# A hand-ordered mixer kernel on one core: new delays for small transfers in its planner, a new order list, sets numbered through the batches

## The chip, the core and the metric

The kernel runs on one core of a Trainium2 chip. Time is device time in microseconds (us) of that core, from one launch. Engines are named as in the profile: PE is TensorE (PEld its weight loads), DVE is VectorE, ACT is ScalarE, POOL is GpSimd, SP is the engine that here only issues transfers. POOL, too, issues transfers, through the software queue.

## The reference

For each of 4 batches, a gated linear attention of 8 heads (sequence 768, head size 48) is followed by a token mixer and a channel mixer with shared weights:

```python
f = 1 / (1 + exp(-f_logit))                       # (B, H, S, D)
for t in range(S):
    state = f[:, :, t, :, None] * state + k[:, :, t] (outer) v[:, :, t]
    y[:, :, t] = q[:, :, t] @ state
x = y as (B, S, H*D)                              # H*D = 384
xt = x.transpose(0, 2, 1)
u = x + (relu(xt @ w_tok1) @ w_tok2).transpose(0, 2, 1)   # 768 -> 256 -> 768
out = u + relu(u @ w_ch1) @ w_ch2                 # 384 -> 1536 -> 384
```

Inputs and output are float32; the kernel computes its matrix products in bfloat16 with float32 accumulation.

## The kernel before, in words

The sequence is cut into 6 chunks of 128 rows. In the text "b.c" is chunk c of batch b, as in sums3.4. For each chunk the kernel makes these steps, each one an entry of a plan:

- gates (L443): ACT takes exp and ln of the loaded f, and DVE or POOL (L457) the low half "Llo" of the logarithm.
- sums (L516): a matmul with a triangle of ones adds the logarithms along the chunk; ACT makes the factors G and Gi (L541, L543), and for batches 1 to 3 "ends" (L550), whose last row a 2 KB transfer "glast" (L556, issued by SP) spreads over the partitions.
- DVE multiplies q and k by the factors (L562) into one of four sets qk. The set is turned (128x128 transposes) into qkT: for batches 0 to 2 on PE (L579) with a copy by DVE or ACT, for batch 3 (TURNED) by a transfer that transposes (L569, issued by SP).
- scores (L476) are made on PE from qkT, and masked into AmT (L616, DVE); "parts" (L492) multiply k by v; DVE carries the running state (L628 to L633), which is copied into state_bd ("sbd", L639) by ACT or POOL.
- y (L651 and L658) makes the chunk's output from state and AmT; it is copied into x_bf and x_nat (L680).

Then the mixer of the batch follows: tok1 (L693), a relu copy, tok2 (L709), the sum (L725) and u_bf (L737); u_bf is turned into uT in two halves "th", on PE (L750) for batches 0 and 1 and by transposing transfers (L739, SP) for batches 2 and 3 (U_TURNED); ch1 (L768) with relu copies into zT (L439 on ACT, L441 on DVE); ch2 (L787), whose sum with x_nat (L793, DVE) is stored by SP (L797), 192 KB at a time. The last tile of the last batch is split into columns 0 to 288 and 288 to 384. x_nat has three buffers, so batch 3 writes into the buffer of batch 0 once that was stored.

Nothing of this runs in the order in which it is written. Every step is added to a list of 1116 entries. ORDER names each entry once, as 4 times its index plus the number of the engine chosen among those that it allows. Plan.best walks through ORDER with prices and landing times written into the entries, chooses a PSUM bank for each user, puts filler matmuls (L834) on PE where it sees PE idle for over 250 ns before 25.5 us, and emits the steps sorted by planned start. On one engine that is the order of ORDER. The planned times are in no instruction: on the chip each engine takes its own list in order, and waits on semaphores for what an instruction needs. So what the plan decides is the order on each engine, the engine of each step, the banks and the fillers.

Entry kinds: ("mm", ...) is PE work, ("el", ...) an elementwise step, ("load", ...) an input transfer, ("fix", own, till) a step that holds its engine for own ns and is done after till ns. Three kinds of ("fix", ...) entries had a fourth number before, by which they took a share of a modelled wire (L235 to L238): glast, the turning transfers and the stores.

Of the kernel before, what the change touches and what calls it, by code (L numbers as in the profile page):

```python
# [20 lines left out]
TURNED = 3  # L21
ORDER = (
# [60 lines left out]
)  # L83
KEPT = 3
SPLIT = 5
SLOTS = (5110, 5800, 7500, 8450, 9600, 10400, 11400, 13000, 14400, 14800, 16700,
         18000, 19100, 19500, 20000, 20700, 21400, 23400, 24300, 25900)
HELD = (2600, 3600, 4100, 4750, 5500, 6500)


class Op:
# [162 lines left out]
def kernel(  # L254
# [25 lines left out]
    def st(shape, dtype, tag):  # L280
        return sb.tile(shape, dtype, tag=tag, name=tag)
# [586 lines left out]
```

## Time and profile before

| what | value |
|---|---|
| runs | 172.79, 171.46, 176.41 us; median 172.79 |
| span of the profiled execution | 170.2 us (the record has its span; a time of its own is not listed) |
| granted TensorE clock in the profile | 1.00 |
| instructions | 4181 |
| PE, DVE, ACT, POOL busy | 162.9, 128.0, 108.2, 99.3 us |
| filler matmuls (L834) | 30 |

The page gives busy time of each engine, the chain of work that ended last, groups of instructions with what ended the idle time before them, and transfers with their time from issue to landing. A matmul's busy time covers its way through the array, so consecutive matmuls overlap in it: how fast PE works is read from the distance of their starts, which the chain of work shows as pieces with a count ("7.80 PE ps L768 x48").

### The profile page before, as it was taken

The page shows a single profiled execution, that of the slowest core. Times are in us where ns is not written, and L with a number is a line of the kernel's source. Part 1 is how long each engine was busy: PE and PEld are TensorE (multiplying, and loading weights), DVE is VectorE, ACT ScalarE, POOL GpSimd, SP SyncE. Part 2 cuts the span into 40 slices and gives each one's busy share as a digit, 9 for nine tenths or more (in the row PEclk, how much of TensorE's full clock was granted, in tenths as well). Part 3 has the DMA queues.
Part 4 walks back from the last instruction along what each step waited for, and adds up shares of the span by engine and source line. Part 5 has one row for each costly group of instructions (what it writes and reads, how often), then busy time and mean ns, then how long its engine had stood idle before and what let it go on. Part 6 is the DMA issues. An engine that isn't in the chain of part 4 may idle for free.

```text
span 170.2 us, 4181 instructions
## 1 busy us (share of the span) xinstructions
PE 162.9 (96%) x1606; PEld 102.8 (60%) x1606; DVE 128.0 (75%) x287; ACT 108.2 (64%) x256; POOL 99.3 (58%) x134
## 2 busy tenths in 40 slices
PE   6899999999999999999999999999999999999992
PEld 2356565665766576665776756665666666566661
DVE  5679995966898998899999868768884723675431
ACT  4759993598879889999999978385545320510100
POOL 7999569896499969999978869603111200000000
PEclk9999999999999999999999999999999999999999
DMA  6999999999999997999998999996920060220253
GB/s 103 141 174 149 156 192 181 212 149 201 192 167 136 161 165 75 116 155 133 182 157 49 134 251 107 144 165 115 228 100 4 0 139 0 92 96 0 78 202 139
DMA packets 102547, 22.71 MB, mean 133 GB/s; under 512 B 95264, under 2 KB 101664, under 8 KB 102528
## 3 DMA queue, kind: packets, MB, share of 16 engines
q0 software_dynamic: 79440, 13.77, 101.8%
q1 hardware_dynamic: 22560, 8.59, 22.5%
q8 instruction: 12, 0.20, 0.5%
q10 hardware_dynamic: 528, 0.10, 0.3%
q14 instruction: 7, 0.06, 0.1%
HBM read 25.17 MB, written 4.72 MB: 176 GB/s over the span
## 4 chain that ended last, share of the span: by engine, by line
PE 64%; DMA 12%; DVE 7%; ACT 6%; POOL 6%; issue 2%; SPq 1%; DVEq 0%; POOLq 0%
PE ps L768 22%; PE ps L787 22%; DMA v_sb<-in_v_dram 5%; PE ps L709 4%; POOL qk_sb L360 4%; PE ps L693 4%; DMA glast<-ends 4%; DMA out_dram<-x_nat 3%; DVE AmT L616 2%; PE ps L476 2%; PE ps L579 2%; PE ps L658 2%; POOL v_sb L360 1%; PE ps L530 1%; PE ps L651 1%
## 5 line engine op out<-in xcount | busy, mean ns | idle before, releaser
L787 PE MATMUL ps<-w_ch,zT 128*128 128x384 bf16 (+2 forms) x300 | 51.6, 320 | 0.0
L768 PE MATMUL ps<-uT,w_ch 128*128 128x384 bf16 x288 | 50.6, 326 | 0.0
L439 ACT ACTIVATE zT<-ps 128x384 bf16<-128x384 f32 x56 | 25.3, 494 | 25.3 <-PE ps L768 25.2
L768 PEld LDWEIGHTS <-w_ch 128*128 128x128 bf16 x288 | 27.7, 98 | 17.7
L787 PEld LDWEIGHTS <-zT 128*128 128x128 bf16 x300 | 27.9, 98 | 16.9
L616 DVE TENSOR_TENSOR AmT<-ps,tri_bf 128x512 bf16<-128x512 f32 x46 | 30.5, 686 | 2.5 <-PE ps L476 2.3
L441 DVE TENSOR_SCALAR zT<-ps 128x384 bf16<-128x384 f32 x40 | 21.1, 554 | 8.8 <-PE ps L768 8.8
L360 POOL DMA_DIRECT2D v_sb<-in_v_dram x24 | 22.2, 925 | 4.1 <-DMA w_ch<-in_moe_w_ch_dram 4.1
L360 POOL DMA_DIRECT2D qk_sb<-in_k_dram x24 | 22.4, 932 | 0.8 <-POOLq L852 0.8
L360 POOL DMA_DIRECT2D qk_sb<-in_q_dram x24 | 22.3, 930 | 0.0
L793 DVE TENSOR_TENSOR x_nat<-x_nat,ps 128x384 f32<-128x384 f32 (+2 forms) x25 | 13.3, 535 | 10.6 <-PE ps L787 10.2
L360 POOL DMA_DIRECT2D f_sb<-in_f_logit_dram x18 | 16.5, 943 | 0.2
L562 DVE TENSOR_TENSOR qk<-qk_sb,GG 128x768 bf16<-128x768 bf16 (+1 forms) x30 | 14.2, 475 | 2.1 <-ACT GG L543 1.0
L450 ACT ACTIVATE f_sb<-f_sb 128x384 f32<-128x384 f32 x24 | 12.5, 524 | 4.6 <-DMA f_sb<-in_f_logit_dram 4.4
L434 POOL CAST state_bd<-state 48x192 bf16<-48x192 f32 x13 | 4.5, 347 | 16.2 <-DVE state L633 14.6
L725 DVE TENSOR_TENSOR x_nat<-x_nat,ps 128x384 f32<-128x384 f32 x21 | 10.5, 550 | 3.4 <-PE ps L709 3.1
L834 PE MATMUL ps<-steady 128*128 128x512 bf16 x30 | 11.3, 483 | 1.7 <-DVE steady L375 1.7
L543 ACT ACTIVATE GG<-ps 128x384 bf16<-128x384 f32 x24 | 11.6, 489 | 2.0 <-PE ps L531 1.9
L541 ACT ACTIVATE GG<-ps 128x384 bf16<-128x384 f32 x24 | 11.7, 488 | 1.4 <-PE ps L531 1.2
L579 PE MATMUL ps<-ident,qk 128*128 128x128 bf16 x144 | 11.6, 224 | 0.0
L579 PEld LDWEIGHTS <-qk 128*128 128x128 bf16 x144 | 9.2, 100 | 2.7 <-DVE qk L562 0.7
L550 ACT ACTIVATE ends<-ps 32x384 f32<-32x384 f32 x15 | 7.0, 481 | 4.9 <-PE ps L531 4.7
(81 smaller groups left out, 234.1 us busy)
## 6 DMA issues: line engine op xcount, KB each, us to landing
out_dram<-x_nat SPq DMA_DIRECT2D x23, 192.0 KB, 3.1
f_sb<-in_f_logit_dram POOLq DMA_DIRECT2D x18, 192.0 KB, 5.4
qk_sb<-in_k_dram POOLq DMA_DIRECT2D x24, 96.0 KB, 5.1
qk_sb<-in_q_dram POOLq DMA_DIRECT2D x24, 96.0 KB, 4.9
v_sb<-in_v_dram POOLq DMA_DIRECT2D x24, 96.0 KB, 5.5
w_ch<-in_moe_w_ch_dram POOLq DMA_DIRECT2D x2, 576.0 KB, 7.5
w_ch<-in_moe_w_ch_dram POOLq DMA_DIRECT2D x1, 1152.0 KB, 10.6
f_sb<-in_f_logit_dram SPq DMA_DIRECT2D x5, 192.0 KB, 4.7
```

What stands on the lines that cost most here:

```text
L360: lambda eng=eng, into=into, of=of: eng.dma_start(out=into, in_=of),
L439: nc.scalar.activation(out_, in_, AF.Relu, bias=0.0, scale=1.0)
L441: nc.vector.tensor_scalar(out_, in_, 0.0, None, ALU.max)
L450: add(ACT, r, lambda: nc.scalar.activation(fb, fb, AF.Exp, bias=0.0, scale=-1.0), make=[key], kind=el, need=([("fb", c)] if c < 1 else []) ...
L541: add(ACT, r, lambda: nc.scalar.activation(G[i], sview(), AF.Exp, bias=0.0, scale=-1.0), make=[("G", i)], bank=p_s, kind=el)
L543: add(ACT, r, lambda: nc.scalar.activation(Gi[i], sview(), AF.Exp, bias=0.0, scale=1.0), make=[("Gi", i)], bank=p_s, kind=el)
L562: add(DVE, r, lambda n=n: nc.vector.tensor_tensor(qk[i4][:, n, :, 0:D], qk_sb[nb][:, n, :, c, :], GG[i][:, n], ALU.mult), need=[(x, nb, c) ...
L579: nc.tensor.transpose(to[:, o + hp, :], blk(src)[:, hp, :], ident)
L616: add(DVE, r, lambda half=half, made=made: nc.vector.tensor_tensor(half, made(), tb4, ALU.mult), need=["tri_bf"], make=[("AmT", i, p)], ba ...
L768: nc.tensor.matmul(banks[pm.at][:, 0:384], lhsT=w[:, kt, c0:c0 + 128], rhs=uT[:, th, :, kt, :], start=(kt == 0), stop=(kt == 2))
L787: nc.tensor.matmul(banks[pm.at][:, 0:n1 - n0], lhsT=zT[:, kt, tt * 128:(tt + 1) * 128], rhs=w_ch2[:, kt, n0:n1], start=(kt == 0), stop=(kt ...
L793: add(DVE, rank("ch2", tt), lambda un=un, pm=pm, n=n1 - n0: nc.vector.tensor_tensor(un, un, banks[pm.at][:, 0:n], ALU.add), make=[("x_nat" ...
```

## The change

The computation is the same, and so are the 1116 entries. The planner's walk no longer keeps a wire for these transfers. A "fix" entry with a fourth number is now only a turning transfer, and a third one starts in the plan no earlier than the last but one is done. glast, stores and turning transfers get fixed delays. The sets qk and qkT (four, as before, now called NQ) are numbered by (b * NCH + c) % NQ in place of c % 4, so with 6 chunks a set comes back after four chunks across the end of a batch, where it came back after two. The "hold" of a bank for scores of batch 3 no longer waits in the plan for the turned set. ORDER is another list, in which 95 of the 1116 entries have another engine.

```diff
+NQ = 4
 ORDER = (
-    184, 0, 20, 24, 28, 44, 48, 176, 56, 60, 64, 72, 76, 80, 84, 92, 96, 100, 104, 112, 144, 4, 12, 52, 68, 204,
...
+    0, 20, 24, 28, 44, 48, 56, 60, 64, 72, 76, 80, 84, 92, 96, 100, 104, 112, 4, 8, 16, 12, 332, 176, 152, 144,
...
+        turned: list = []
...
+            if op.kind[0] == "fix" and len(op.kind) > 3 and len(turned) > 1:
+                t = max(t, turned[-2])
...
-            elif op.kind[0] == "fix" and len(op.kind) > 3:
-                wire = max(wire, t + 1000) + op.kind[3]
-                if op.kind[3] > 1000:
-                    op.end = max(op.end, wire + 1200)
+            elif len(op.kind) > 3 and op.kind[0] == "fix":
+                turned.append(op.end)
...
-        need = [("qkT", c % 4, p) for c in cs for p in range(2)]
+        need = [("qkT", (b * NCH + c) % NQ, p) for c in cs for p in range(2)]
...
-        i, i4, nb, g4 = c % 2, c % 4, b % NB, (b * NCH + c) % 4
+        i, i4, nb, g4 = c % 2, (b * NCH + c) % NQ, b % NB, (b * NCH + c) % 4
...
-                kind=("fix", 600, (5200, 5200, 3400)[b - 1], 300))
+                kind=("fix", 500, (6000, 5200, 4500)[b - 1]))
...
+            add(SP, r, lambda: nc.sync.dma_start_transpose(out=qkT[i4], in_=qk[i4].rearrange("t n h d -> t (n h d)")),
+                need=[("qh", i4), ("kh", i4)], make=[("qkT", i4, 0), ("qkT", i4, 1)], kind=("fix", 1350, 6500, 1))
             hold = Bank()
-            add(SP, r, lambda: nc.sync.dma_start_transpose(out=qkT[i4], in_=qk[i4].rearrange("t n h d -> t (n h d)")),
-                need=[("qh", i4), ("kh", i4)], make=[("qkT", i4, 0), ("qkT", i4, 1)], kind=("fix", 1900, 6000, 1700))
-            add(PE, r, lambda: None, need=[("qkT", i4, 0)], make=[("hold", b, c)], bank=hold, kind=("mm", 1))
+            add(PE, r, lambda: None, make=[("hold", b, c)], bank=hold, kind=("mm", 1))
...
-                make=[("uT", 3 * th + j, d) for j in range(3) for d in range(3)], kind=("fix", 1900, 6000 if b > 2 else 8000, 1900))
+                make=[("uT", 3 * th + j, d) for j in range(3) for d in range(3)], kind=("fix", 1400, 4000 if b > 2 else 7200, 1))
...
-                    need=[("x_nat", xn, tt, n0) if end else ("x_nat", xn, tt)], kind=("fix", 350, 2000, 580))
+                    need=[("x_nat", xn, tt, n0) if end else ("x_nat", xn, tt)], kind=("fix", 420, 4500 if b < 3 else 2000))
```

Decoded with the entry list, ORDER gives these sequences at the places of which the prediction speaks (before, then after; "ld" is a load issued by POOL, "store0.3" the store of tile 3 of batch 0, "ch2_3 t2" the three entries of one tile).

```
POOL, first 26 entries: the same in both (k, q, v of batch 0, w_tok1, w_tok2)
POOL, batch 3, before: ld k3.4, Llo3.2, u_bf x3, ld q3.4, ld v3.4, ld k3.5, ld q3.5, Llo3.5, Llo3.4, sbd3.0 x2, sbd3.1 x2, ld v3.5
POOL, batch 3, after:  u_bf, ld k3.4, u_bf x3, Llo3.5, ld q3.4, sbd3.0, Llo3.4, ld v3.4, ld k3.5, sbd3.0, ld q3.5, sbd3.1, ld v3.5, sbd3.1
PE, start, before: parts0.3 scores0.3 sums0.5 turns0.4 y0.2 y0.3 turns0.5 scores0.4 parts0.4 scores0.5 tok1 x4 y0.4 y0.5 tok1 x8 tok2
PE, start, after:  parts0.3 scores0.3 sums0.5 y0.2 turns0.4 turnk0.5 y0.3 turnq0.5 scores0.4 parts0.4 scores0.5 tok1 y0.4 tok1 x2 y0.5 tok1 x9 tok2
PE, batch 3 tok2, before: t5 t1 t2 t0 t3 ch2 t4 ch2 x12, then ch1_3 (th 0 first)
PE, batch 3 tok2, after:  t3 t5 ch2 t4 ch2 ch2 t2 t0 t1 ch2 x6, then ch1_3 (six of th 1 first)
SP, before: ... qkT3.4 qkT3.5 store1.5 store0.2 store1.0 store1.3 store0.3 store0.5 uT3 th0 uT3 th1 stores
SP, after:  ... store0.2 qkT3.5 qkT3.4 glast3.4 uT3 th1 uT3 th0 stores (five of batch 1, six of batch 2, those of batch 3)
PE, last entries, before: ch2_3 t4 (end), t5 columns 0-288, t5 columns 288-384
PE, last entries, after:  ch2_3 t1 (end), t2
```

More of the change, by code (lines that the diff above doesn't have):

```diff
@@ L300 @@
     G, Gi = [t[:, 0] for t in GG], [t[:, 1] for t in GG]
-    qk = [st([128, 2, H, 64], BF16, f"qk{i}") for i in range(4)]
+    qk = [st([128, 2, H, 64], BF16, f"qk{i}") for i in range(NQ)]
     qh, kh = [t[:, 0] for t in qk], [t[:, 1] for t in qk]
-    qkT = [st([128, 8, 128], BF16, f"qkT{i}") for i in range(4)]
+    qkT = [st([128, 8, 128], BF16, f"qkT{i}") for i in range(NQ)]
     AmT = [st([128, 8, 128], BF16, f"AmT{i}") for i in range(2)]
@@ L411 @@
         once(DVE, lambda i=i: nc.vector.memset(state_bd[i], 0.0), [("sbd", i)], 220)
-    for i in range(4):
-        once(DVE, lambda i=i: nc.vector.memset(ends[i][96:128, :, D:64], 1.0), [("ends", i)], 200)
+    for i in range(NQ):
+        if i < 4:
+            once(DVE, lambda i=i: nc.vector.memset(ends[i][96:128, :, D:64], 1.0), [("ends", i)], 200)
         for n, tl in (("qh", qh[i]), ("kh", kh[i])):
@@ L480, in attention @@
             own = 212 if k else 330
-            chain = add(PE, due(b, cs[0]), lambda c=c, k=k: scores(c % 4, heads[k]), need=need, bank=heads[k][1],
+            chain = add(PE, due(b, cs[0]), lambda c=c, k=k: scores((b * NCH + c) % NQ, heads[k]), need=need, bank=heads[k][1],
                         kind=("mm", own if live and b else own + 107, own), tail_of=chain)
@@ L491, in parts @@
                     hp, par = h // 2, h % 2
-                    nc.tensor.matmul(dg(k)[par * 64:par * 64 + 64, hp, :], lhsT=kh[c % 4][:, h, :],
+                    nc.tensor.matmul(dg(k)[par * 64:par * 64 + 64, hp, :], lhsT=kh[(b * NCH + c) % NQ][:, h, :],
                                      rhs=v_sb[nb][:, h, c, :], start=b > 0 or (c == 0 and hp == 0), stop=True,
@@ L496, in attention @@
         if live and b == 0:
-            add(PE, due(b, cs[0]), parts, need=[("kh", cs[0] % 4), ("v", nb, cs[0])], make=["sums"], bank=p_d,
+            add(PE, due(b, cs[0]), parts, need=[("kh", cs[0] % NQ), ("v", nb, cs[0])], make=["sums"], bank=p_d,
                 kind=("mm", 345, 238))
         elif live:
-            chain = add(PE, due(b, cs[0]), parts, need=[("kh", c % 4) for c in live] + [("v", nb, c) for c in live],
+            chain = add(PE, due(b, cs[0]), parts, need=[("kh", (b * NCH + c) % NQ) for c in live] + [("v", nb, c) for c in live],
                         bank=p_d, kind=("mm", 230 + 115 * len(live), 123 + 115 * len(live)), tail_of=chain)
@@ L597, in rest @@
     def rest(b, c, r, p_a, p_d, dg):
-        i, i4, nb, g4 = c % 2, c % 4, b % NB, (b * NCH + c) % 4
+        i, i4, nb, g4 = c % 2, (b * NCH + c) % NQ, b % NB, (b * NCH + c) % 4
         last = c == NCH - 1
```

118 rows, old and new, of the table ORDER are left out of this document.

## The prediction, made before the changed kernel ran

> **What bounds the kernel now.** I read the page first, then busy time by stretches of the span, then the chain of waits in order of time, and last single places: the groups, the transfers and the lists of POOL, DVE and SP around batch 3.
>
> ```profile
> span 170.2 us, 4181 instructions
> PE 162.9 (96%) x1606; PEld 102.8 (60%) x1606; DVE 128.0 (75%) x287; ACT 108.2 (64%) x256; POOL 99.3 (58%) x134
> ```
>
> PE bounds the run. Next come the stretches: start and end, length, then busy time and count of PE, PEld, DVE, ACT, POOL, and the granted clock.
>
> ```profile
> 0.00:19.85 19.85, 17.37 (x175) 8.95 (x175) 15.26 (x52) 13.52 (x34) 17.32 (x28) 1.00 1.90 142
> 19.85:32.20 12.35, 11.68 (x154) 7.85 (x155) 10.18 (x25) 9.15 (x22) 10.09 (x14) 1.00 1.34 200
> 32.20:143.40 111.20, 110.44 (x1125) 71.47 (x1123) 89.07 (x186) 81.69 (x193) 71.92 (x93) 1.00 1.36 133
> 143.40:167.30 23.90, 23.43 (x156) 14.52 (x154) 13.51 (x27) 3.81 (x8) 0.00 (x0) 1.00 0.27 99
> ```
>
> I cut where the chain (start, length, what) changes its kind:
>
> ```profile
> 11.54 8.27 DMA v_sb<-in_v_dram
> ...
> 20.81 0.80 PE ps L519 x2
> ...
> 24.61 0.75 PE ps L834 x3
> 25.37 0.65 PE ps L693 x4
> 26.02 0.17 PE ps L651 x4
> 26.19 0.20 PE ps L658 x8
> ```
>
> ```profile
> 32.22 7.80 PE ps L768 x48
> ...
> 83.36 0.89 PE ps L579 x16
> ...
> 107.42 0.55 PE ps L476 x16
> 107.97 0.36 PE ps L492 x16
> ...
> 120.47 5.31 DMA out_dram<-x_nat
> ...
> 126.50 0.50 ACT x_bf L430
> ...
> 160.30 6.54 PE ps L787 x52
> 166.87 0.26 DVE x_nat L793
> ```
>
> Until 19.85 the run waits for v of chunk 3 of batch 0 (8.27 us on the way). From 32.2 on PE is nearly without holes: idle is 111.20 - 110.44 = 0.76 us and then 23.90 - 23.43 = 0.47. Busy time hides short holes, so I also count by starts. 7.80/48 gives 162 ns for a 384-column matmul, 0.89/16 gives 56 ns for a turn, and 34, 23, 41 and 25 ns follow in the same way for L476, L492, L651 and L658. After 19.85 the lists hold 708 of the first (115.0 us), 148 turns (8.2), 168 scores (5.8), 136 parts (3.1), 76 and 176 matmuls of y (3.1 and 4.4), and the two fp32 sums 0.8: 140.4 us. The way from 19.85 to 167.3 is 147.4. So 7.0 us is all that any order could give back there: 3 of it before 32.2 (12.35 less 9.3 of work at these prices), 4 after.
>
> **The change part by part.** The delays, the wire and the limit of two turns in flight are in no instruction. They cost nothing by themselves; on the chip act only the lists of the engines, the banks, the fillers and the set numbers.
>
> *The start, up to 19.85: 0.* The first 26 entries of POOL are the same, so v arrives by the same queue, and the PE list holds the same set of steps ahead of parts0.3. From below and above I allow 0.5 us for transfers that land otherwise.
>
> *Fillers.* Their number comes from the plan:
>
> ```profile
> L834 PE MATMUL ps<-steady 128*128 128x512 bf16 x30 | 11.3, 483 | 1.7 <-DVE steady L375 1.7
> ```
>
> Most lie ahead of 19.85, under the loads. The three shown at 24.61 last 0.25 each. Two more or fewer at a place where PE has work make 0.5 us either way; I take 0.
>
> *19.85 to 32.2: +0.2 (from -0.8 to +0.8).* y0.4 needs the mask that POOL finishes here:
>
> ```profile
> 25.13 0.63 POOL L611 TENSOR_SCALAR_AFFINE_SELECT AmT<-AmT 128x512 bf16<-128x512 bf16 x1 [0.75 <-ACT AmT L608]
> ```
>
> It ends at 25.76. Before, four tok1 (0.65) fill the wait for it; in the new list only one stands ahead of y0.4, two between y0.4 and y0.5. So three tok1, 0.5 us, move behind the wait. Against it, ACT has one copy in place of two ahead of its part of that mask, which I take for 0.3. The rest of the stretch has the same steps; the new tok1 ends with two matmuls of the other half where one stood, which covers 0.16 us more of the relu.
>
> *The sets numbered through the batches: 0.* The multiply into a set would wait for PE if a set were short. It waits for ACT alone:
>
> ```profile
> DVE qk L562 <- ACT GG L543: 1.0, 2, 0.6
> ```
>
> More distance removes no wait that is there, and four sets stay four.
>
> *Batch 0's stores ahead of batch 3: -0.3 (from -0.6 to 0).* The old SP list has store0.3 and store0.5 behind turned sets and stores of batch 1; a landing 5.31 us later released x_nat, x_bf and then y of batch 3, which is the chain at 120.47 above:
>
> ```profile
> DVE x_nat L432 <- DMA out_dram<-x_nat: 0.6, 1, 0.6
> ```
>
> In the new list all of batch 0 is stored ahead of qkT3.5, so this wait goes. Five stores of batch 1 now stand behind uT3, which nobody waits for, because x_nat of batch 1 isn't written again. PE had little idle there; next late are the same copies by their queue on DVE.
>
> *The loads of chunk 5 of batch 3: +0.7 (from 0 to +1.8).* This is the wait that I see added. Rows of POOL before, then the landing times (min, median, max) of the two q and one k loads issued from 103 to 107, then the multiply that uses the last of them
>
> ```profile
> 105.37 0.89 POOL L360 DMA_DIRECT2D qk_sb<-in_k_dram  x1
> 106.24 0.90 POOL L360 DMA_DIRECT2D qk_sb<-in_q_dram  x1
> 107.13 1.65 POOL L457 TENSOR_TENSOR Llo<-f_sb 128x384 bf16<-128x384 f32 x2
> 110.07 0.72 POOL L434 CAST state_bd<-state 48x192 bf16<-48x192 f32 x2 [1.29 <-DVE state L628]
> ```
>
> ```profile
> DMA to landing us min/median/max: 4.6/7.7/7.8
> ```
>
> ```profile
> 115.67 0.55 DVE L562 TENSOR_TENSOR qk<-qk_sb,GG 128x768 bf16<-128x768 bf16 x1
> ```
>
> and y3.2 on PE:
>
> ```profile
> 123.38 0.33 PE L651 MATMUL ps<-state_bd,qkT 128*128 128x96 bf16 x4
> ```
>
> In the new list the first sbd3.0, Llo3.4, the loads v3.4 and k3.5 and the second sbd3.0 stand ahead of q3.5. From 110.07, when state is there, they take 0.36 + 0.83 + 0.9 + 0.9 + 0.36 = 3.3 us, so q3.5 is issued at 113.4, not 106.2, and lands between 118.0 and 121.2. On DVE its multiply stands directly ahead of the copies of y3.1, of relus, state3.1 and the masks of chunk 2: about 3.4 us of work that y3.2 needs. y3.2 stands after the same PE work in both lists, at 123.4. DVE is free for that work at about 118.6 to 121.8, and done at 122.0 to 125.2: PE waits 0 to 1.8 us. The median landing would give 1.7; the four turning transfers that crowd the queue at 105 to 116 are mostly over by then, so I take 0.7. Behind the same multiply wait qkT3.5, qkT3.4 and glast3.4 on SP; scores3.4 is 3.4 us of PE work later than y3.2, which covers them. The Trainium skill (DMA: Bandwidth & Descriptors, "Anatomy of one DMA") gives 2.0 us plus bytes over 436 GB/s per transfer, 2.2 us for such a 96 KB load, an estimate by that page; then nothing would be late and the sum would be 0.7 lower. The rows above, 4.6 and more, speak against it under this load.
>
> *Two Llo of batch 2 move from DVE to POOL, other engines change in 93 entries: 0 (from -1.5 to +1.5).* The totals stay: DVE has 282 entries for 285, ACT 256 for 257, POOL 136 for 132. The holes after 32.2 are 4 us; the bounds are that they close by some third or grow by as much.
>
> *The end: +0.6 (from +0.4 to +1.2).* The last PE work was 96 columns of tile 5, now it is all of tile 2. The groups of the last sum, then the stores of the last 26 us:
>
> ```profile
> L793 DVE TENSOR_TENSOR x_nat<-x_nat,ps 128x384 f32<-128x384 f32 x23 | 12.6, 550 | 10.1 <-PE ps L787 9.7
> ...
> L793 DVE TENSOR_TENSOR x_nat<-x_nat,ps 128x96 f32<-128x96 f32 x1 | 0.3, 255 | 0.1
> ```
>
> ```profile
> out_dram<-x_nat SPq DMA_DIRECT2D x12, 192.0 KB, 1.9
> ...
> out_dram<-x_nat SPq DMA_DIRECT2D x1, 48.0 KB, 1.6
> ```
>
> The sum takes 0.55 for 0.255, the store 1.9 for 1.6; eight stores crowd the last 4 us, which gives the upper end.
>
> Sum: 0.2 - 0.3 + 0.7 + 0.6 = +1.2 us, a span of 171.4. The median of the runs lies 2.6 above the span shown (the lowest 1.3); I add to the median: 172.79 + 1.2 = **174.0 us**.
>
> **The rivals.** *The new list closes holes.* For it: 7.0 us are open. Against it: they are spread, and no wait of PE is long. If the added wait doesn't come and 2 us of holes close, 172.79 + 0.5 - 2.0 = 171.3, chance 0.22. Over 2% faster needs 3.5 us, half of all holes; chance 0.05, near 169.
>
> *q3.5 is late in full*: 1.1 more than taken, 175.1, chance 0.12; it stays inside 2%.
>
> *The turned tiles of batch 3 come late, and the kernel is slower.* SP's rows, the landing of all four such transfers, and the tok2 ahead of the first:
>
> ```profile
> 135.99 3.25 SPq L739 DMA_TRANSPOSE uT<-u_bf x2
> ```
>
> ```profile
> DMA to landing us min/median/max: 2.8/2.8/7.2
> ```
>
> ```profile
> 133.00 1.62 PE ps L709 x10
> ```
>
> tok2 ended at 134.6, the first issue came 1.4 later. In the new list eight ch2 entries (0.65) and three tok2 (0.33) lie between the last tok2 of half 1 and its first ch1: 6.2 us, where 9.1 lay for the first half before. So a landing over 6.2 - 1.4 = 4.8 us decides; at 7.2 PE waits 2.4 us and the time is 174.0 + 2.4 = 176.4. For it: 7.2 was seen once. Against it: that was amid loads, and at 136 both took 2.8. Chance 0.13. The Trainium skill (TensorE: Matmul & The Clock Gate, Part 1) says that about 3.4 us of idle PE halves its clock; by it this wait would stay just short, and one of 3.4 us would cost some 1.7 more, an estimate by that page. The granted clock is 1.00 in every stretch here, so no row shows it.
>
> **How the numbers follow.** The forecast has 0.48: all of its terms together. Faster by over 2% (about what a measurement of this kernel can tell from no change): 0.05. Slower by over 2%, above 176.25: the late tiles' 0.13, and 0.04 of the forecast's upper end, 0.17. The rest, 0.78, is within 2%. The range reaches from 171.4, the smaller gain, to 176.8, the late tiles with 0.4 of the crowded end on top; the forecast's own is 172.5 to 175.5.
>
> **What would show it.** Right: the chain has no store ahead of x_nat of batch 3; POOL issues q3.5 after a state_bd of batch 3, and the multiply behind it on DVE waits for a transfer; the last sum takes 0.55 us. Wrong: PE idle over 1 us at the uT3 tiles, or a wait of batch 1 or 2 that takes more than 1 us; a first ch1 well before or after 32.2.

## The result, and the profile after

| | before | changed |
|---|---|---|
| median of five runs | 172.79 us | 176.78 us (176.40 to 178.44) |
| ratio to the kernel before | | 1.029, 95% interval 1.023 to 1.035 |
| span of the profiled execution | 170.2 us | 176.7 us |
| first ch1 starts at | 32.06 us | 34.27 us |
| from there to the end of the span | 138.12 us | 142.46 us |

The changed kernel is slower by 4.0 us; forecast were 1.2. Executions over 1.5% above the fastest of their kernel are in the medians here and are left out of the ratios. From here on lines of the kernel are those of the changed one, two or three above those of the kernel before (L771 is ch1, L790 ch2, L582 the turns, L654 the part of y made from the state, L696 tok1, L565 the multiply of q and k, L619 the mask AmT, L636 the state, L460 Llo, L362 the loads, L444 a relu copy on DVE).

The page of the changed kernel:

```profile
span 176.7 us, 4175 instructions
...
PE 162.4 (92%) x1604; PEld 101.1 (57%) x1604; DVE 130.4 (74%) x284; ACT 108.4 (61%) x255; POOL 102.4 (58%) x138
```

PE does the same work in 6.5 us more of span. This execution took 178.44 us, the longest of the five, so 6.5 us is more than the change cost. Then four stretches as before the change; the first two cuts stand at the same steps (parts0.3, first ch1), the third at the same time, 143.4; columns are start and end, length, busy time of PE, PEld, DVE, ACT and POOL, granted clock, DMA:

```profile
0.00:21.68 21.68, 15.63 (x174) 7.77 (x174) 14.10 (x45) 16.01 (x39) 17.68 (x29) 1.00 1.88 144
21.68:34.27 12.59, 11.74 (x153) 7.77 (x153) 10.48 (x27) 7.91 (x19) 9.82 (x13) 1.00 1.33 188
34.27:143.40 109.13, 105.52 (x1089) 67.50 (x1087) 90.58 (x183) 77.98 (x184) 73.42 (x94) 1.00 1.36 122
143.40:173.00 29.60, 29.53 (x194) 18.05 (x192) 14.75 (x31) 6.49 (x14) 1.48 (x3) 1.00 0.34 111
```

Two stretches are to be looked at: the first, 1.8 us longer, and the third, where PE is idle for 109.13 - 105.52 = 3.6 us; the kernel before had 0.76 there. The waits of PE by name (total, times, longest):

```profile
PE ps L582 <- DVE qk L565: 3.1, 4, 2.0
...
PE ps L771 <- DVE zT L444: 1.6, 1, 1.6
...
PE ps L654 <- DVE AmT L619: 0.7, 1, 0.7
PE ps L696 <- DVE AmT L619: 0.7, 1, 0.7
```

The 3.1 us of L582 lie in the start, the other three in the long stretch. A hole is the distance of two matmul starts less what the columns of the first take, 160 ns for 384 (scores start closer than that and count against the sum of the smaller holes). The way from the first ch1 to the end divides into the columns, the long holes, the sum of everything else between the starts, and the end; the last column is a mended kernel, told below:

| us | before | changed | e9 |
|---|---|---|---|
| holes over 0.25 us | 1.24 | 4.52 | 1.17 |
| smaller holes, in sum | 2.48 | 3.10 | 3.88 |
| start of the last matmul to the end | 3.56 | 4.13 | 3.66 |
| the whole way | 138.12 | 142.46 | 139.55 |

The six holes over 0.25 us of the changed kernel begin at 67.2 (0.85), 74.2 (0.36), 82.9 (0.38), 92.8 (0.30), 97.1 (0.83) and 123.9 us (1.80). The three of the kernel before were at 55.3 (0.55), 65.5 (0.28) and 126.5 (0.41). About 2.5 us of the smaller holes are in every column: nine times PE goes from wide matmuls to scores, on to parts and back to wide ones, and each of these three passages costs 0.09 to 0.10 us.

**What is seen at 64 to 68 us.** POOL and DVE of the changed kernel, and y1.4 of PE, which waits:

```profile
64.15 0.83 POOL L460 TENSOR_TENSOR Llo<-L 128x384 bf16<-128x384 f32 x1 [2.30 <-ACT L L455]
64.20 0.99 DVE L636 TENSOR_TENSOR state<-tsum,glast 128x192 f32<-128x192 f32 x1
...
66.46 0.82 POOL L460 TENSOR_TENSOR Llo<-L 128x384 bf16<-128x384 f32 x1 [0.61 <-ACT L L455]
66.57 0.93 DVE L636 TENSOR_TENSOR state<-tsum,glast 128x192 f32<-128x192 f32 x1
...
68.16 0.34 PE L654 MATMUL ps<-state_bd,qkT 128*128 128x96 bf16 x4 [0.69 <-DVE AmT L619]
```

The state, 128x192 with both operands in SBUF, takes 0.99 and 0.93 us where 0.35 is usual, and ends 0.2 us after POOL's Llo does. The group of L636 from 34 us on (minimum, median, maximum in ns) of the kernel before, where it is L633, and of the changed one:

```profile
L633 DVE TENSOR_TENSOR state<-tsum,glast x12: 348/354/364, 51.8 to 128.0; 128x192 f32<-128x192 f32 x12
```

```profile
L636 DVE TENSOR_TENSOR state<-tsum,glast x12: 347/357/1427, 51.0 to 136.0; 128x192 f32<-128x192 f32 x12
```

The third long one takes 1.43 us, and a multiply L565, also all in SBUF, takes 1.07 for 0.55:

```profile
81.56 0.82 POOL L460 TENSOR_TENSOR Llo<-L 128x384 bf16<-128x384 f32 x1
81.73 1.07 DVE L565 TENSOR_TENSOR qk<-qk_sb,GG 128x768 bf16<-128x768 bf16 x1
...
95.99 1.43 DVE L636 TENSOR_TENSOR state<-tsum,glast 128x192 f32<-128x192 f32 x1
...
96.35 0.84 POOL L460 TENSOR_TENSOR Llo<-f_sb 128x384 bf16<-128x384 f32 x1
```

Masks (0.68 us) and relus (0.55), which have an input in PSUM, keep their time beside an Llo. The holes at 67, 83 and 97 follow these four places. The hole at 74 does not: PE waits there for a copy u_bf by ACT, and it is there with 0.36 us in every run that has the new order. Nor is the one at 93 at such a place.

**What is seen at 124 us.** POOL from 113 us, the landing time of the last of these loads, and the multiply and the ch1 that wait:

```profile
113.33 0.82 POOL L460 TENSOR_TENSOR Llo<-f_sb 128x384 bf16<-128x384 f32 x1 [2.68 <-ACT f_sb L455]
114.10 0.92 POOL L362 DMA_DIRECT2D qk_sb<-in_q_dram  x1
...
118.58 0.88 POOL L362 DMA_DIRECT2D qk_sb<-in_q_dram  x1
...
120.98 0.56 DVE L444 TENSOR_SCALAR zT<-ps 128x384 bf16<-128x384 f32 x1
...
124.32 0.56 DVE L565 TENSOR_TENSOR qk<-qk_sb,GG 128x768 bf16<-128x768 bf16 x1 [2.79 <-ACT zT L442]
...
125.87 1.14 PE L771 MATMUL ps<-uT,w_ch 128*128 128x384 bf16 x6 [1.63 <-DVE zT L444]
```

```profile
DMA to landing us min/median/max: 5.6/5.6/5.6
```

q of chunk 5 is issued at 118.58 and lands at 118.58 + 5.6 = 124.2; DVE stands from 121.5 to 124.32 ahead of its multiply, with the zT that PE needs queued behind it. The line names an ACT relu as what ended DVE's wait; whether that or the load did is what e1 asks.

### The profile page after: what moved, and what is told of

Its sections match the earlier page's. It is cut to its first block, busy times and chain, and to the rows that moved or that the text cites. A ratio compares the mean times of both kernels' runs of the same rounds, so it can differ in the third digit from the quotient of the medians.

```text
span 176.7 us, 4175 instructions
## 1 busy us (share of the span) xinstructions
PE 162.4 (92%) x1604; PEld 101.1 (57%) x1604; DVE 130.4 (74%) x284; ACT 108.4 (61%) x255; POOL 102.4 (58%) x138
## 5 line engine op out<-in xcount | busy, mean ns | idle before, releaser
L771 PE MATMUL ps<-uT,w_ch 128*128 128x384 bf16 x288 | 51.4, 326 | 1.8 <-DVE zT L444 1.6
L790 PE MATMUL ps<-w_ch,zT 128*128 128x384 bf16 (+2 forms) x300 | 52.9, 319 | 0.0
L771 PEld LDWEIGHTS <-w_ch 128*128 128x128 bf16 x288 | 27.4, 98 | 19.3 <-issue 2.5
L790 PEld LDWEIGHTS <-zT 128*128 128x128 bf16 x300 | 27.9, 98 | 17.3 <-issue 0.5
L442 ACT ACTIVATE zT<-ps 128x384 bf16<-128x384 f32 x53 | 24.3, 495 | 20.1 <-PE ps L771 20.0
L619 DVE TENSOR_TENSOR AmT<-ps,tri_bf 128x512 bf16<-128x512 f32 x46 | 30.3, 681 | 2.9 <-PE ps L479 2.9
L444 DVE TENSOR_SCALAR zT<-ps 128x384 bf16<-128x384 f32 x43 | 22.7, 552 | 10.1 <-PE ps L771 10.0
L362 POOL DMA_DIRECT2D v_sb<-in_v_dram x24 | 22.0, 918 | 5.8 <-DMA w_ch<-in_moe_w_ch_dram 3.9
L362 POOL DMA_DIRECT2D qk_sb<-in_k_dram x24 | 22.1, 921 | 0.8 <-POOLq L855 0.8
L362 POOL DMA_DIRECT2D qk_sb<-in_q_dram x24 | 22.1, 921 | 0.0
L565 DVE TENSOR_TENSOR qk<-qk_sb,GG 128x768 bf16<-128x768 bf16 (+1 forms) x30 | 14.9, 502 | 8.3 <-ACT zT L442 2.8
L362 POOL DMA_DIRECT2D f_sb<-in_f_logit_dram x18 | 16.5, 924 | 0.3 <-issue 0.2
L582 PE MATMUL ps<-ident,qk 128*128 128x128 bf16 x144 | 11.5, 220 | 3.2 <-DVE qk L565 3.1
L582 PEld LDWEIGHTS <-qk 128*128 128x128 bf16 x144 | 8.7, 98 | 7.4 <-DVE qk L565 6.0
L696 PE MATMUL ps<-x_bf,w_tok 128*128 128x384 bf16 x48 | 11.5, 325 | 0.7 <-DVE AmT L619 0.7
L837 PE MATMUL ps<-steady 128*128 128x512 bf16 x28 | 9.4, 443 | 1.7 <-DVE steady L377 1.7
```

The source lines that it names most:

```text
L362: lambda eng=eng, into=into, of=of: eng.dma_start(out=into, in_=of),
L442: nc.scalar.activation(out_, in_, AF.Relu, bias=0.0, scale=1.0)
L444: nc.vector.tensor_scalar(out_, in_, 0.0, None, ALU.max)
L565: add(DVE, r, lambda n=n: nc.vector.tensor_tensor(qk[i4][:, n, :, 0:D], qk_sb[nb][:, n, :, c, :], GG[i][:, n], ALU.mult), need=[(x, nb, c) ...
L582: nc.tensor.transpose(to[:, o + hp, :], blk(src)[:, hp, :], ident)
L619: add(DVE, r, lambda half=half, made=made: nc.vector.tensor_tensor(half, made(), tb4, ALU.mult), need=["tri_bf"], make=[("AmT", i, p)], ba ...
```

## Experiments

In e1, e2, e5, e7 and e10 every PSUM bank is fixed to the one that the changed kernel's plan gives, and the lists of PE, ACT and SP are its own, so that only the named edit differs. Ratios are to the kernel before, run beside them; where "from the first ch1" stands, it is the way from there to the end of the span in the profiled execution.

**e1: the four loads moved ahead** (codes of ORDER: 2040, 2044, 2048, 2052 are q3.4, v3.4, k3.5, q3.5; 3564 is Llo3.5).

```diff
-    3688, 3564, 2040, 3900, 3660, 3552, 2044, 2048, 3664, 2052, 3176,
+    3688, 2040, 2044, 2048, 2052, 3564, 3900, 3660, 3552, 3664, 3176,
```

> The changed kernel with one edit: on POOL the four loads q and v of chunk 4 and k and q of chunk 5 of batch 3 stand ahead of the Llo of chunk 5, as in the kernel before; every other list and every PSUM bank is that of the changed kernel. Theory A (the load of q of chunk 5 is late, DVE stands at the multiply L565 until it lands at 124.1 us, and PE waits 1.6 us for the next zT): the load lands by about 117, the PE wait before L771 at 124 goes, and the time falls from 176.8 by 1.2 to 1.8 us, to 175.0 to 175.6. Rival B (ACT's zT at 123.8 is what is late, as the wait names it, and the load only happens to land beside it): the PE wait stays over 1 us and the time is 176.8 within 0.5. Rival C (Llo of chunks 4 and 5, now issued later by four loads of 0.9 us, comes late instead): a wait of PE at L534 or L582 of 1 us or more takes its place, and the time is 176.3 to 177.5.

Measured: 175.87 us, ratio 1.020 (1.016 to 1.025); 141.25 us from the first ch1 to the end, 1.2 less. POOL and DVE:

```profile
112.91 0.90 POOL L362 DMA_DIRECT2D qk_sb<-in_q_dram  x1
...
114.88 0.85 POOL L460 TENSOR_TENSOR Llo<-f_sb 128x384 bf16<-128x384 f32 x1
114.96 1.20 DVE L565 TENSOR_TENSOR qk<-qk_sb,GG 128x768 bf16<-128x768 bf16 x1
...
116.81 1.14 PE L771 MATMUL ps<-uT,w_ch 128*128 128x384 bf16 x6 [0.34 <-DVE AmT L619]
...
121.71 0.55 DVE L565 TENSOR_TENSOR qk<-qk_sb,GG 128x768 bf16<-128x768 bf16 x1
```

The last multiply no longer waits, and the hole of 1.80 us at 124 is gone. So it was the load, not the relu that the wait named: the relu's list was not touched. The load landed later than I expected (112.91 + 6.4 = 119.3), still in time. An Llo, moved by the loads, now meets another multiply (1.20 us for 0.55) and costs PE 0.50 at 116.1, which eats a third of the gain. The time alone would not prove this: it is 0.3 us above the range of theory A, and its interval touches that of the changed kernel.

**e2: four Llo from POOL to DVE** (2569, 2557, 2605 and 3504 are Llo2.1, Llo2.0, Llo2.4 and Llo3.0; the last digit chooses the engine).

```diff
-        on = (DVE, DVE, (DVE, POOL), POOL)[b]
+        on = (DVE, DVE, (DVE, POOL), (POOL, DVE))[b]
-    2569, 2557, 2605, 3504
+    2568, 2556, 2604, 3505
```

> The changed kernel with one edit: four of the Llo subtractions that POOL has (chunks 0, 1 and 4 of batch 2, chunk 0 of batch 3) run on DVE at the same place of the order; every other list and every PSUM bank is that of the changed kernel. Theory A (a DVE instruction whose operands are all in SBUF, L636 or L565, stands still while POOL does an Llo: L636 took 0.99, 0.93 and 1.43 us against 0.36 elsewhere, L565 1.07 against 0.55): no L636 is over 0.45 us beside these places, the PE waits for AmT at 67.2 (0.85 us), 82.9 (0.38) and 97.1 (0.83) shrink to under half, and the time falls from 176.8 by 0.8 to 1.8 us, to 175.0 to 176.0. Rival B (DVE is simply full from 60 to 100 us, busy 9.5 to 10.0 us of each 10): four more instructions of 0.55 us on DVE make the same waits as long or longer, and the time is 176.5 to 178.5.

Measured: 176.18 us, ratio 1.025 (1.020 to 1.030); 142.04 us from the first ch1. The group of L636 and, at 64 us, the new wait:

```profile
L636 DVE TENSOR_TENSOR state<-tsum,glast x12: 345/348/358, 49.3 to 133.9; 128x192 f32<-128x192 f32 x12
```

```profile
64.05 0.56 DVE L460 TENSOR_TENSOR Llo<-L 128x384 bf16<-128x384 f32 x1 [0.74 <-ACT L L455]
...
65.26 0.48 PE L696 MATMUL ps<-x_bf,w_tok 128*128 128x384 bf16 x2 [1.04 <-DVE AmT L619]
```

No state is long any more, the holes at 83, 93 and 97 are gone and the one of 0.85 has shrunk to 0.26, although DVE has four subtractions of 0.56 us more to do: Rival B, a full DVE, falls. But Llo2.0, now ahead of two masks on DVE, waits there for ACT's logarithm, and a new hole of 1.21 us stands just ahead. The edit had made its own wait, and the time missed the range of theory A by 0.2.

**e5: only two of them, Llo2.4 and Llo3.0** (2605 to 2604, 3504 to 3505, with the line of e2).

> The changed kernel with one edit: two Llo subtractions of POOL, chunk 4 of batch 2 and chunk 0 of batch 3, run on DVE at the same place of the order; all else, banks too, as in the changed kernel. Measured from the first ch1 to the end, so that the landings of the start stay out: 142.5 us in the changed kernel, 138.1 in the kernel before. Theory A (these two hold up a DVE instruction that has all its operands in SBUF: L565 at 81.7 for 0.5 us, L636 at 96.0 for 1.1): the PE waits at 82.9, 92.8 and 97.1 (0.38, 0.30, 0.83 us) go, as they did when four Llo were moved, while the wait of 1.2 us at 64 that came with the other two doesn't: 140.9 to 141.3, and the time about 175.3. Rival B (the waits there come of a full DVE, and went because the earlier wait had let DVE catch up): 142.0 to 143.0, time 176.8.

Measured: 176.51 us, ratio 1.025 (1.019 to 1.030); 143.3 us from the first ch1. The three holes are gone, 1.51 us in all, and yet the way is longer. PE's waits after 34 us, then three stretches around the wait that is left, with the granted clock as the third number from the end:

```profile
PE ps L771 <- DVE zT L444: 2.1, 1, 2.1
PE ps L654 <- DVE AmT L619: 0.7, 1, 0.7
```

```profile
121.00:124.00 3.00, 0.89 (x6) 0.41 (x5) 1.86 (x4) 1.64 (x4) 0.00 (x0) 1.00 0.21 21
124.00:128.00 4.00, 4.00 (x44) 2.35 (x42) 3.24 (x8) 0.49 (x1) 1.51 (x3) 0.57 1.15 126
128.00:130.00 2.00, 2.00 (x24) 1.35 (x23) 1.64 (x5) 1.64 (x4) 0.69 (x2) 1.00 1.13 71
```

PE came to the place earlier, but the load's time is set by POOL, so the hole grew from 1.80 to 2.28 us; and in the 4 us after it the mean granted clock was 0.57. My number failed because I had taken the gains for independent. The median also hides two kinds of executions: three of the six, the profiled one among them, have a mean granted clock of 0.99 and took 177.1 to 177.8 us, the other three 1.00 and 175.7 to 175.9, which is near the 175.3 of theory A.

**e10: the same four Llo made memsets**, which only write; the low part of the logarithm is left out for these chunks.

```diff
+        idle_lo = (b, c) in ((2, 0), (2, 1), (2, 4), (3, 0))
-        op.fn = lambda: (nc.vector if op.engine == DVE else nc.gpsimd).tensor_tensor(lo, full, hi, ALU.subtract)
+        op.fn = lambda: nc.gpsimd.memset(lo, 0.0) if idle_lo else (nc.vector if op.engine == DVE else nc.gpsimd).tensor_tensor(lo, full, hi, ALU.subtract)
```

> The changed kernel with the four Llo that met a DVE instruction (chunks 0, 1 and 4 of batch 2, chunk 0 of batch 3) replaced on POOL by a memset of the same tile to 0, at the same place with the same waits: the low part of the logarithm of these four chunks is left out of the computation. All lists but POOL's, and all banks, are those of the changed kernel. Theory A (DVE stands still because POOL reads two operands of SBUF; an instruction that only writes doesn't stop it, or is too short to): L636 is 0.36 us and L565 0.55 beside these places, the PE waits at 67, 83, 93 and 97 go to under 0.4 us each, 141.0 us from the first ch1 to the end but for what the wait for the load at 124 grows by, and the time falls from 176.8 by 0.5 to 1.5. Rival B (it is DVE's own load, which no memset on POOL changes): the waits stay, 142.2 to 142.8 us, time 176.8 within 0.5. Rival C (any POOL instruction that works on SBUF stops DVE for its length): L636 is over 0.5 us by about what the memset lasts.

Measured: 175.83 us, ratio 1.016 (1.011 to 1.021); 142.3 us from the first ch1. Two of the places:

```profile
62.31 0.59 POOL L460 MEMSET Llo<- 128x384 bf16 x1
62.52 0.35 DVE L636 TENSOR_TENSOR state<-tsum,glast 128x192 f32<-128x192 f32 x1
...
78.64 0.52 POOL L460 MEMSET Llo<- 128x384 bf16 x1
78.95 0.55 DVE L565 TENSOR_TENSOR qk<-qk_sb,GG 128x768 bf16<-128x768 bf16 x1
```

Both DVE instructions begin inside a memset and keep their time. The holes at 67, 83 and 97, 2.06 us in all, are gone with DVE's list untouched; the one at 93 stays (0.29), so what POOL reads does not make it. The one at 124 grew to 2.79 us, and the clock behind it halved, as in e5:

```profile
122.50:126.00 3.50, 3.29 (x38) 1.78 (x37) 1.98 (x6) 0.49 (x1) 1.50 (x3) 0.54 1.26 153
```

The profiled execution took 176.64 us; the three of the six with a mean granted clock of 1.00 took 174.1 to 175.1. Rivals B and C fall. The Trainium skill (SBUF — State Buffer, "SBUF: two separate sides") says that DVE and GpSimd share a pair of ports held by one instruction at a time, and that a DVE instruction with two SBUF inputs meets it only against a GpSimd instruction that reads SBUF. The rows here agree: 0.93 to 1.43 us beside a subtraction, 0.35 beside a memset.

**e3: the start of the kernel before** in the changed kernel: in ORDER the entries of batch 0 up to its turns uT0 (three late sums of x_nat apart) come first, in the old order with the old engines, then the rest as in the changed kernel; banks and fillers follow the plan.

> The changed kernel with the start of the kernel before: the lists of all engines up to the first matmul of ch1 of batch 0 (loads, gates, attention, tok1, tok2 and the turns of batch 0, with their choice of engine) are those of the kernel before, the rest is that of the changed kernel; banks and fillers follow the plan. Theory A (the new order of the start costs time by itself): the first ch1 is at 32.0 to 33.0 us where the changed kernel has 34.3, and the time falls from 176.8 by 1.2 to 2.3 us, to 174.5 to 175.6. Rival B (the loads of batch 0 landed 0.3 to 3.6 us later in that one profile by chance, with the same issues, and the order of the start is as good): the first ch1 is at the same place as in the changed kernel within what the landings move, and the time is 176.8 within 0.6.

Measured: 176.74 us, ratio 1.028 (1.022 to 1.034), first ch1 at 32.49. Theory A falls: its place fits, but the time doesn't fall, and from the first ch1 on it is 142.48 us as in the changed kernel. The mirror of this run, e4 (the kernel before with the changed kernel's start), could not be built and gives nothing.

**e11: the changed kernel again.**

> The changed kernel once more. If the place of the first ch1 goes by how the loads of the start land and not by the lists, it differs from the 34.3 us of the first profile by 0.5 us or more (32.5 to 33.0 where three kernels with the same start lists had 32.5, 32.6, 32.7), and the stretch from the first ch1 to the end is 142.5 us within 0.3 again. If the start lists themselves set it, 34.3 within 0.4. Time 176.0 to 177.2.

Measured: 175.98 us, ratio 1.022 (1.019 to 1.026), first ch1 at 31.99 us. The same lists gave 34.27 and 31.99. The load of q of chunk 3 of batch 0, issued by POOL at 10.6 us in the profiles of the kernel before, the changed kernel and e11, took

```profile
DMA to landing us min/median/max: 6.0/6.0/6.0
```

```profile
DMA to landing us min/median/max: 9.6/9.6/9.6
```

```profile
DMA to landing us min/median/max: 7.1/7.1/7.1
```

from issue to landing. So Rival B of e3 stands: the start varies by over 2 us from one execution to the next, and the new list is not worse there by an amount that these runs show. The old order varies as much: 32.06 us in the kernel before, 34.78 in e8 below. From the first ch1 on e11 took 141.8 us, 0.7 less than I expected: at 79.4 DVE came first this time, and POOL was held up instead, off PE's path,

```profile
79.42 0.55 DVE L565 TENSOR_TENSOR qk<-qk_sb,GG 128x768 bf16<-128x768 bf16 x1
79.49 1.16 POOL L460 TENSOR_TENSOR Llo<-L 128x384 bf16<-128x384 f32 x1 [0.28 <-ACT L L455]
```

and the meeting at 93 (96.0 in the first profile) cost 0.6 for 1.1. In these rows whoever starts first goes through and the other waits. The state at 95.99 above is an exception that no run explains: it starts 0.36 us ahead of the Llo and takes 1.43 all the same.

**e6: the last 96 columns last again** (codes 4444, 4448, 4452, 4456, 4460 at the end of ORDER).

> The changed kernel with one edit: the last 96 columns of the last tile (three groups of ch2, their sum on DVE, their store) come last on PE, DVE and SP, as in the kernel before, in place of a tile of 384 columns; banks follow the plan. Theory A (the smaller last sum and store shorten the end): from the last matmul to the end 3.3 to 3.5 us where the changed kernel has 3.8, and the time falls by 0.3 to 0.6, to 176.3. Rival B (the end is set by something that doesn't go by size): 3.7 to 3.9, no change.

Measured: 176.50 us, ratio 1.024 (1.019 to 1.029). From the last matmul's end to the end of the span 3.48 us for 3.80, from its start 3.69 for 4.13, of which 0.12 is only that the last matmul has 96 columns in place of 384. Theory A holds for the end; the time can't tell 0.3 us. The hole at 122 was 2.16 us here, and the clock after it stayed:

```profile
125.00:129.00 4.00, 4.00 (x62) 2.63 (x61) 3.54 (x9) 1.97 (x5) 1.88 (x5) 1.00 1.27 125
```

**e8: the old order in the new code.** ORDER alone is that of the kernel before.

> The kernel before with the numbering of the sets through the batches, the new delays of the plan and its limit on turns, but its own order. Theory A (all that was lost is in the order): 138.1 us from the first ch1 to the end within 0.4, and the time that of the kernel before within 0.6 us. Rival B (the numbering makes a set come free later, and with it a transposition on the SP queue or a multiply L565): a wait of over 0.5 us at L565 or before L479 that the kernel before hasn't, and the time 0.8 to 3 us above it.

Measured: 172.40 us, ratio 0.998 (0.994 to 1.002); 138.2 us from the first ch1. Theory A: numbering, delays and the limit cost nothing that shows; all of the loss is in the order, with the banks and fillers that the plan takes from it.

**e7: both mends.** The loads of e1; Llo2.4, Llo3.0, Llo2.1 and also Llo3.4 (the one that met the multiply in e1) on DVE; Llo2.0 on DVE behind the masks of y1.5.

```diff
-    2569, 2557, 2605, 3504, 3552
+    2568, 2604, 3505, 3553
-    1948,
+    1948, 2556,
```

> The changed kernel with both mends and no other: the four loads of batch 3 ahead of the Llo of chunk 5, and five Llo on DVE (chunks 0, 1, 4 of batch 2 and 0, 4 of batch 3), of which chunk 0 of batch 2 stands behind the AmT of chunk 5 of batch 1, so that DVE doesn't wait there for ACT's logarithm; PE, ACT, SP lists and all banks as in the changed kernel. Theory A (the late load and the Llo on POOL beside DVE are the whole of what was lost after the first ch1, the end apart): PE waits over 0.3 us after the first ch1 sum to under 1.2 us where the changed kernel has 4.5, from the first ch1 to the end 138.3 to 139.3 us, and the time 172.8 to 173.8. Rival B (DVE, with 2.8 us more to do, is late elsewhere): new PE waits for DVE of 1.5 us or more in all, 140.0 to 142.0 from the first ch1 to the end, time 174.5 to 176.5.

**e9: the same with the end of e6.**

> The changed kernel with the four loads of batch 3 moved ahead, the five Llo on DVE, and the last 96 columns of the last tile last; banks follow the plan. Theory A (three terms that add: load, Llo on POOL, end): 139.7 us from the first ch1 to the end with the first two mends, 0.44 less with the end, so 139.0 to 139.5, and the time 0.5 to 1.2% above the kernel before (173.6 to 174.8). Rival B (what is left after the first two mends is one cause that also hides the end): 139.6 or more, time 174.7 or more.

Measured: e7 174.74 us, ratio 1.012 (1.008 to 1.017), 139.7 us from the first ch1; e9 173.68 us, ratio 1.010 (1.006 to 1.013), 139.55 us. All waits of PE in e9 after 33 us:

```profile
PE ps L696 <- DVE x_bf L435: 0.3, 1, 0.3
PE ps L534 <- DVE Llo L460: 0.2, 1, 0.2
PE ps L753 <- ACT u_bf L433: 0.2, 1, 0.2
```

The long holes are down to 1.17 us, as theory A said, and the interval of e9 lies clear below both of the changed kernel's. But e7 missed: its way is 0.4 us over theory A, its time lies in the range of Rival B, and e9 is still 1.4 us over the kernel before, because the smaller holes have grown from 2.48 to 3.88 us (table above). Nine of them are of 0.14 to 0.23 us, where the kernel before has two and the changed kernel five; where the profile names a releaser, it is a mask on DVE or a copy on ACT. I didn't follow them further. The end is shorter by 0.46 us in e9 (4.12 in e7, 3.66 in e9), the whole way by 0.14: the smaller holes are 0.2 larger (3.68 in e7), and 0.12 are columns that now stand ahead of the last matmul. No version here beats the kernel before.

## Why the prediction was wrong

- **Start, 0 and +0.2**: right as far as the runs show (e3, e11, e8). The 2.2 us that the first profile has there are landings of that execution, and "a first ch1 well after 32.2" was no sign against the forecast, since I had not bounded how much the start varies.
- **Numbering: 0**: right (e8, 0.998). **Fillers: 0**: the changed kernel has 28 for 30, all ahead of the first ch1, so they are part of the start; no run has them alone.
- **Batch 0's stores, -0.3**: right; the hole of 0.41 at 126.5 us has no counterpart in the changed kernel.
- **Loads of chunk 5, +0.7 (0 to 1.8)**: the mechanism was right, the size not: 1.80 us, the upper end, by e1. I had q3.5 issued at 113.4; it was at 118.58. I let POOL start from its state_bd at 110.07, but in the new list Llo3.5 and q3.4 stand ahead of them all, and Llo3.5 waited until 113.33 for ACT; then the two state_bd, Llo3.4, v3.4 and k3.5 came in front. And PE stood at a ch1, for a relu on DVE, and not at y3.2.
- **"Two Llo of batch 2 move from DVE to POOL, other engines change in 93 entries: 0 (from -1.5 to +1.5)"**: this step failed. The long holes other than the one at 124 sum to 2.72 us, for 0.83 before the change, and the smaller holes grew by 0.6: +2.5, past the bound of 1.5. The runs showed in its place that POOL's Llo stops those DVE instructions that read two SBUF operands (e2, e5, e10), 0.5 to 1.1 us at a time, with masks for PE queued behind. That is shown for the holes at 67, 83 and 97, 2.06 of the 2.72 us; of the other two, 0.66 us, the one at 74 is in every run with the new order and the one at 93 stayed in e10. I looked at totals of engines, which hardly moved; three of the four Llo were on POOL before, too, and only their place against DVE changed. The kernel before has no such meeting after 32 us: its state L633 is never over 0.364 us, its multiply L562 never over 0.565. Not all of it comes back with the mend: e7, with the load moved too, is 2.8 us shorter than the changed kernel from the first ch1, of which the load's hole is 1.8; that leaves about 1.0 for moving the Llo.
- **End, +0.6**: right. From the start of the last matmul it is 0.57 us in the profile and 0.44 by e6; without the 0.12 for its columns, 0.45 and 0.32.
- **The rivals**: the holes didn't close, they grew. There was also less to close: of the 7.0 us counted as open, 4 lay after 32.2, and about 2.5 of these are the passages to scores and parts, which every run here has. The turned tiles of batch 3 landed 2.8 us after issue and PE did not wait for them. The time came near that rival's, 176.4, for another reason, and that it lies just under the end of the range, 176.8, is luck.

The terms as measured, -0.4 + 1.8 + 2.5 + 0.45 = 4.35 us, against 4.34 in the way from the first ch1 to the end and 4.0 and 3.7 us in the medians of two comparisons. What stays open are the small holes, and with them what the Llo cost in whole.

## What to carry to other kernels

Where PE is nearly full, an order is judged by who runs beside whom: look for DVE instructions with both inputs in SBUF next to POOL instructions that read SBUF, and for a transfer's wait that stands at the head of an engine's list, by its issue time and not by its neighbours. A late load fixes the time of all that follows: gains ahead of it only make the wait longer (e5, e10), so mend it first. And where the start varies with landings, compare from the first step that no load sets.

## What the runs showed of the hardware that I had not expected

- Holes of PE of 1.74, 1.80, 1.95, 2.00 and 2.16 us at 121 to 124 us (e3, the first profile, e2, e11, e6) left the granted clock at 1.00; after holes of 2.28 (e5) and 2.79 us (e10) at the same place it was halved for 3.4 us. Length alone does not decide: in the start of e1 a hole of 1.15 us, in a stretch in which PE did little else (busy 0.69 us from 7.0 to 9.0), was followed by a clock of 0.50, too. The prediction drew on the Trainium skill (TensorE: Matmul & The Clock Gate, Part 1) for 3.4 us of idle; here 2.28 were enough, and the measurement decides. In e5 that cost about 2 us beside the hole: the smaller holes, among which slow matmuls count, sum to 5.05 us there for 3.10 in the changed kernel.
- The loser of a meeting of POOL and DVE is not always DVE: an Llo that starts 0.07 to 0.14 us after the multiply takes 1.15 to 1.16 us for 0.82 (e11 at 79.49, the changed kernel at 115.33).
- One load of 96 KB with the same issue time, in three executions (kernel before, e11, changed kernel), took 6.0, 7.1 and 9.6 us.
